# A new written order for the recurrence of a gated linear-attention and mixture-of-experts kernel, with ten more fill products

## Chip, cores, metric

One core of one Trainium2 chip. The metric is device microseconds (us) of one execution; lower is better. The engines are TensorE (PE; its weight loads are PEld), VectorE (DVE), ScalarE (ACT), GpSimd (POOL) and SyncE (SP), which here only issues DMAs.

## What is computed

```python
f = sigmoid(f_logit)                      # (B, H, S, D) = (4, 8, 768, 48), float32
for t in range(S):                        # one 48x48 state per batch and head
    state = f[t][:, None] * state + outer(k[t], v[t])
    y[t]  = q[t] @ state
x = y as (B*S, H*D) = (3072, 384)
e = argmax(x @ w_gate)                    # 8 experts, w1: 384x1024, w2: 1024x384
out = softmax(x @ w_gate)[e] * (relu(x @ w1[e]) @ w2[e])
```

## The kernel before, in words

**Units.** The recurrence is done in chunks of 128 tokens. Twelve units (0 to 11) hold one chunk of two batches each; even units and odd units follow each other in time through a state. Each unit has 8 segments of 128 partitions x 128 tokens: half `a` is segments 0 to 3, `b` is 4 to 7, and `c` to `f` are quarters (c, d make a; e, f make b). For a unit, ACT computes `exp` and `ln` of the logits (L684, L693), DVE a running sum (`sum`, L700), ACT two exponentials of it (`r`, L715/L717; `dec`, L730). The keys are multiplied by `r` (on POOL as `kr`, on DVE as `krv`, both L721), the queries by `dec` on DVE (`q`, L743). PE turns the keys (`kp`, L650 into tile tr), makes scores (`sc`, L647 into s), DVE masks them (`mx`, L775), PE multiplies them into the values (`wi`, L647 into yt), adds the older state's share (`bef`) and makes the unit's own state (`dp`); ACT copies turned keys out of PSUM (`keep`, L786), and the outputs (`set`, L857); DVE and POOL update the state (`upd`, L846/L848; with p, L850).

**Routing.** PE turns the outputs back to token rows (`xp`, `lay` on ACT copies them, L942), makes logits (`lo`), DVE picks the expert (`lg`, `oh`, `place`, `rec`), PE counts (`cnt`), and POOL scatters 128 rows at a time to their expert's region in memory (`send`, L260). `soon`, `turn`, `wide` load, turn and multiply the first rows of experts 0 and 1 ahead of time. Behind the recurrence come two second products of those rows (L456), then the experts, one after another, with weights loaded two ahead.

**What sets the order.** Nothing is scheduled by a planner at run time: `FIRST_STEPS` (L552) is a text of steps that the loop at L1106 carries out one by one, and every engine gets its instructions in the order of that text and runs them in that order. A step that waits holds up all that stands behind it on its engine. Loads (`lf`, `lk`, `lq`, `lv` of a unit; `lw`, `lww` first and second weights of an expert; `consts0` the 32 KB mask, `consts1` the other constants) are issued by SP in the text's order, each behind the last ACT step that stands before it in the text (`paced`, L657). `fill16` is 16 products of a zero tile into a bank that is written anew later (`warm`, L950): they compute nothing. A product of 128x128 float32 shows as two PE records.

**Buffers that tie engines together.** Scores go to two PSUM banks in turn, `kp`, `dp`, `xp` and `cnt` to a ring of two (L629), so each waits until the reader of the one before last (ACT's `keep` or `lay`, DVE's `upd` or `lg`) is done. The buffer of `r` is single.

```python
def paced(load):
    if "act" in done:
        tc.add_manual_dep(load.ins, done["act"].name, SYNC, ...)
def warm(count):
    for _ in range(count):
        nc.tensor.matmul(yt[0][:, 0], lhsT=pad[:, 0:C], rhs=pad[:, 0:C], start=True, stop=True)
for what, u, part in re.findall(r"([a-z]+)(\d+)([a-fp]?)", FIRST_STEPS):
    DO[what](int(u), part)
```

Of the kernel before, what the change touches and what calls it, by code (L numbers as in the profile page):

```python
# [170 lines left out]
def kernel(  # L171
# [366 lines left out]
    def load_pads(e):  # L538
# [11 lines left out]
        tc.add_to_no_dep_group("xs", ins)  # L550

    FIRST_STEPS = """  # L552
        lf0d lf1a lf0f lf0c lf0e lk0a exp0d ln0d lf1b lq0a lk0b sum0d exp1a ln1a exp0c exp0f
        exp0e consts0 lq0b lf2 ln0c sum0c ln0f sum0f sum1a ln0e sum0e lq1 exp1b lf3 r0c fill16
        r0f fill8 dec0f krv0c kp0c ln1b r0d sum1b dec0c lv0 r0e krv0d dec0e lk1 q0f krv0e dec1a
        q0c lv1 exp2 krv0f kp0d q0e dec0d q0d ln2 keep0a r1a sel0 lf4 r1b kp0e q1a kp0f keep0b
        lk2 sc0c sc0d sc0e last0 sc0f lk3 dec1b exp3 ln3 dp0 lq2 sum2 dec2 mx0a mx0b wi0a set0a
        lf5 kr1a kp1a upd0 last1 gate0 q1b consts1 sum3 kr1b kp1b r2 keep1a keep1b exp4 kr2b
        sc1a sc1b wi0b set0b lv2 lv3 ln4 kr2a dp1 mx1a wi1a set1a last2 line0 xp0b mx1b wi1b lq3
        upd1 lay0b q2 upd1p line1 line2 line3 line4 kp2b dec3 last3 lf6 sum4 set1b kp2a keep2a  # L560
        keep2b lq4 sc2a mx2a sc2b r3 xp0a xp1a lo1 wi2a mx2b krv3 lg1 lay0a lk4 wi2b q3 upd0p
        dp2 exp5 bef2 ln5 sum5 lq5 lay1a dec4 sc3a upd2 q4 mx3a kp3b lf7 exp6 line5 kp3a lk5
        sc3b set2a keep3b last4 r4 keep3a mx3b dp3 upd3 upd2p lv4 xp1b lv5 dec5 wi3a lk6 q5
        set2b wi3b ln6 kr4a kp4a lay1b kr4b r5 keep4a kr5a kp4b sc4a lf8 sum6 sc4b exp7 keep4b
        mx4a xp2b mx4b bef3 lk7 ln7 sum7 sc5a lq6 last5 lq7 lay2b kr5b sc5b r6 kr6b dp4 set3a
        kr6a lf9 set3b lv6 xp3a upd4 exp8 lo3 kp5b mx5a pads0 lg3 wi4a wi4b dec6 q6 last6 upd4p
        lay3a keep5b oh3 dec7 q7 lf10 r7 kr7b kp5a xp3b lay3b bef4 keep5a sc6a lk8 cnt3 ex3
        set4b mx5b place3 kr7a lq8 upd3p mx6a rec3 lv7 last7 ln8 xp2a set4a sc6b lay2a dp5 exp9
        upd5 send0 wi5a kp6a kp6b wi5b bef5 lk9 lq9 ln9 sum8 keep6b keep6a dp6 sum9 dec8 send0
        last8 lf11 sc7a upd6 set5a kp7b set5b mx6b r8 kp7a wi6a keep7b upd5p q8 keep7a lw0 wi6b  # L570
        upd6p send0 kr8b exp10 xp4a send0 xp5a ln10 mx7a lay4a lo5 lg5 dec9 sc7b oh5 lay5a bef6
        set6a xp4b lay4b xp5b kr8a mx7b wi7a q9 lay5b set6b lv8 r9 exp11 cnt5 place5 send0 lv9
        ex5 dp7 upd7 wi7b ln11 kr9a upd7p sc8a kp8b keep8b mx8a send0 kp8a lk10 bef7 sc8b sc9a
        lq11 set7a rec5 send0 xp6b keep8a line6 line7 dp8 lay6b sum10 kr9b wi8a mx8b send0 upd8
        set7b lk11 lq10 xp6a lay6a kp9a wi8b keep9a r10 mx9a xp7a sum11 lv10 kp9b send0 keep9b
        lo7 bef8 sc9b dec11 upd8p lg7 lay7a send0 oh7 lww0 lv11 mx9b kr10a dp9 send0 set8b kr10b
        xp7b set8a wi9a upd9 wi9b send0 dec10 soon0 lay7b q10 cnt7 line8 line9 ex7 xp8a lay8a
        bef9 set9a sc10a lw1 set9b sc10b place7 r11 q11 xp8b mx10a kr11b xp9a lo9 lay8b rec7
        send0 kr11a xp9b mx10b lg9 lay9b wi10a send0 wi10b bef10 set10a oh9 sc11a lay9a sc11b
        set10b cnt9 send0 mx11a mx11b xp10a lo10 turn0 last9 upd9p line10 send0 wi11a lg10  # L580
        place9 oh10 lay10a wi11b bef11 set11a ex9 rec9 xp10b lay10b send0 wide0 cnt10 send0
        set11b ex10 rec10 place10 xp11a lww1 line11 lo11 send0 xp11b lay11a lay11b turn1 lg11
        oh11 send0 ex11 rec11 wide1 send0 cnt11 last10 last11 place11 send0 wide2 send0 wide3
        send0
    """

    with ExitStack() as st:
# [1222 lines left out]
```

## Time and profile before

| | |
|---|---|
| runs | 359.98, 360.91, 361.52 us (median 360.91) |
| profiled execution | 362.03 us, of which the span of the trace is 360.3 us |
| recurrence and routing | to about 126 us of the span; then the experts |
| mean granted TensorE clock | 0.987 |

Times in the rows below are us from the start of the span. A timeline row gives start, duration, engine, line, operation, tiles written<-read, shape and count (x), and in brackets the idle time of the engine before it with what ended it.

### The profile page before, as it was taken

How to read it: one execution, taken by the hardware profiler on the slowest of the kernel's cores; microseconds unless marked ns; L12 is line 12 of the kernel's file. 1: busy time of each engine (PE TensorE's matmuls, PEld its weight loads, DVE VectorE, ACT ScalarE, POOL GpSimd, SP SyncE). 2: the span in 40 equal slices, each digit the busy share in tenths (PEclk: the TensorE clock that was granted, in tenths of full speed). 3: DMA queues.
4: the chain of work that ended last, by engine and by line, in shares of the span. 5: the costliest groups of instructions: out<-in, count | busy, mean ns of one | idle time of the engine just before them, and what ended most of it. 6: DMA issues, size and time to landing. Idle time of an engine off the chain costs nothing.

```text
span 360.3 us, 10263 instructions
## 1 busy us (share of the span) xinstructions
PE 344.2 (96%) x3962; PEld 295.4 (82%) x3962; DVE 275.7 (77%) x487; ACT 172.9 (48%) x372; POOL 247.5 (69%) x273
## 2 busy tenths in 40 slices
PE   8699998999999999999999999999999999999993
PEld 8488887888889868999997797896996896599682
DVE  5899989888984847489677858868978967977840
ACT  6999897876623211551443254155245234335310
POOL 6064785785875689699997499399485989935122
PEclk9799999999999999999999999999999999999998
DMA  6999879788948944999982899799179999980241
GB/s 196 359 324 351 291 256 358 262 295 315 323 130 279 366 116 116 311 291 371 391 300 64 268 387 338 216 365 376 36 183 384 226 349 389 372 305 17 70 153 47
DMA packets 57352, 94.97 MB, mean 264 GB/s; under 512 B 21016, under 2 KB 41307, under 8 KB 56272
## 3 DMA queue, kind: packets, MB, share of 16 engines
q1 hardware_dynamic: 54128, 84.60, 70.9%
q0 software_dynamic: 3168, 9.64, 7.0%
q8 instruction: 33, 0.54, 0.6%
q14 instruction: 23, 0.19, 0.2%
HBM read 79.22 MB, written 15.21 MB: 262 GB/s over the span
## 4 chain that ended last, share of the span: by engine, by line
PE 74%; DMA 8%; POOL 7%; issue 3%; ACT 3%; DVE 1%; SPq 1%; another core or an unknown queue 1%; POOLq 0%; ACTq 0%
PE hps L1404 15%; PE yps L1462 14%; PE yt L647 9%; PE tr L650 6%; PE yps L1279 6%; PE s L647 5%; DMA w2t<-in_moe_w_dram 4%; PE tr L647 4%; PE hps L436 3%; POOL was L1307 3%; PE hps L1256 2%; PE hps L1462 2%; DMA w1t<-in_moe_w_dram 2%; POOL w1t L1307 2%; POOL wsum L1298 2%
## 5 line engine op out<-in xcount | busy, mean ns | idle before, releaser
L260 POOL DMA_INDIRECT out_dram<-ysb,dst x26 | 28.5, 1096 | 48.2 <-DVE ysb L1480 22.5
L1422 ACT ACTIVATE hT<-hT 128x352 f32<-128x352 f32 (+1 forms) x48 | 23.9, 506 | 38.3 <-DVE hT L1392 38.1
L260 POOL DMA_INDIRECT xs<-xr,posi x24 | 27.4, 1140 | 19.0 <-issue 6.0
L1462 PE MATMUL yps<-w2t,hT 128*128 128x192 f32 x224 | 39.1, 328 | 0.0
L1462 PEld LDWEIGHTS yps<-w2t,hT 128*128 128x128 f32 x224 | 36.6, 190 | 3.0 <-issue 2.5
L1404 PE MATMUL hps<-xbs,w1t 128*128 128x176 f32 (+2 forms) x216 | 35.7, 309 | 0.3 <-POOL w1t L1307 0.3
L1307 POOL TENSOR_TENSOR was<-w1t 128x256 f32<-128x256 f32 x35 | 29.6, 863 | 7.4 <-DMA w1t<-in_moe_w_dram 3.8
L721 POOL TENSOR_TENSOR k<-k,r 128x512 f32<-128x512 f32 x20 | 28.3, 1424 | 8.6 <-ACT r L717 5.3
L1392 DVE TENSOR_TENSOR hT<-hps,hT 128x352 f32<-128x352 f32 (+1 forms) x42 | 22.2, 529 | 15.5 <-PE hps L1404 9.9
L1404 PEld LDWEIGHTS hps<-xbs,w1t 128*128 128x128 f32 x216 | 32.5, 190 | 0.6 <-issue 0.5
L1415 ACT COPY hT<-hps 128x352 f32<-128x352 f32 (+1 forms) x54 | 24.8, 459 | 16.7 <-PE hps L1404 4.7
L775 DVE COPY_PREDICATED at<-mpack,s 128x1024 f32<-128x1024 uint8 x24 | 31.1, 1316 | 1.6 <-PE s L647 1.5
L700 DVE TENSOR_TENSOR_SCAN sum<-g,cap 128x1032 f32<-128x1032 f32 (+2 forms) x16 | 27.7, 1754 | 3.9 <-ACT g L693 3.9
L1279 PE MATMUL yps<-qw,hqT 128*32 128x192 f32 (+1 forms) x192 | 27.5, 381 | 0.4 <-issue 0.2
L1307 POOL TENSOR_TENSOR w1t<-w1t 128x256 f32<-128x256 f32 x28 | 25.9, 925 | 0.6
L647 PE MATMUL yt<-at,v 128*48 128x128 f32 x384 | 24.3, 275 | 0.1
L647 PE MATMUL s<-q,k 64*64 64x128 f32 (+1 forms) x768 | 23.0, 261 | 0.9 <-issue 0.8
L647 PEld LDWEIGHTS s<-q,k 64*64 64x64 f32 x768 | 20.7, 141 | 3.0 <-issue 2.5
L1404 PE MATMUL hps<-xbs,was 128*128 128x176 f32 (+2 forms) x120 | 21.5, 310 | 0.5 <-ACT hold L1415 0.5
L647 PEld LDWEIGHTS yt<-at,v 128*48 128x48 f32 x384 | 20.2, 123 | 2.1 <-issue 1.2
L1279 PE MATMUL yps<-w2t,hT 128*32 128x384 f32 x192 | 21.4, 487 | 0.0
L1476 ACT ACTIVATE held<-yps,tg 128x192 f32<-128x192 f32 x24 | 10.1, 420 | 21.7 <-PE yps L1462 21.7
(187 smaller groups left out, 857.5 us busy)
## 6 DMA issues: line engine op xcount, KB each, us to landing
w1t<-in_moe_w_dram SPq DMA_DIRECT2D x8, 1536.0 KB
w2t<-in_moe_w_dram SPq DMA_DIRECT2D x8, 1536.0 KB
qw<-in_moe_w_dram SPq DMA_DIRECT2D x16, 768.0 KB
qw<-in_moe_w_dram SPq DMA_DIRECT2D x8, 1536.0 KB
q<-in_qu_dram SPq DMA_DIRECT2D x11, 512.0 KB
k<-in_ku_dram SPq DMA_DIRECT2D x11, 512.0 KB
f<-in_fu_dram SPq DMA_DIRECT2D x10, 512.0 KB
xs<-pad SPq DMA_DIRECT2D x8, 600.0 KB
```

What stands on the lines that cost most here:

```text
L260: ins = nc.gpsimd.indirect_dma_start(out=dst, out_offset=bass.IndirectOffsetOnAxis(ap=idx, axis=0), in_=src, in_offset=None, bounds_check= ...
L647: done["pe"] = nc.tensor.matmul(*a, **k).ins
L700: nc.vector.tensor_tensor_scan(x["sum"][:, part].rearrange("p s c -> p (s c)"), x["g"][:, part].rearrange("p s c -> p (s c)"), cap[:, part ...
L721: ins = on.tensor_tensor(k, k, units[u]["r"][:, part], op=OP.mult).ins
L775: nc.vector.copy_predicated(all_of(x["at"][:, a]), causal, all_of(x["ps", a]))
L1279: nc.tensor.matmul(yp[r], lhsT=h[:, f, at : at + T], rhs=w[:, f, cols], start=f == order[0], stop=f == order[-1], skip_group_check=True,)
L1307: on.tensor_tensor(to, first[1], second[1], op=op)
L1392: nc.vector.tensor_tensor(place(to), one, place(other), op=op)
L1404: nc.tensor.matmul(banks[n][:, g], lhsT=lhs[:, C * g : C * g + C], rhs=rhs, start=op == "new" and g == 0, stop=True, skip_group_check=True,)
L1415: nc.scalar.copy(place(more[0]), banks[n])
L1422: nc.scalar.activation(place(n), place(n), AF.Relu, scale=scale)
L1462: nc.tensor.matmul(to, lhsT=h[:, f], rhs=w[:, f], start=start and f == 0, stop=f == HB - 1, skip_group_check=True,)
```

## The change

Only the text `FIRST_STEPS` changes. All steps are the same and on the same engines, but in another order on every queue; `fill8` becomes `fill14`, and two steps `fill2` are new, so 34 products of zeros instead of 24. What stands first on each engine, before and after:

```
PE before   fill16 fill8 kp0c kp0d kp0e kp0f sc0c sc0d sc0e sc0f dp0 wi0a kp1a kp1b sc1a sc1b wi0b dp1 wi1a xp0b wi1b
PE after    fill16 fill14 kp0c fill2 sc0c fill2 sc0d kp0e kp0d kp0f sc0e sc0f dp0 kp1a wi0a kp1b wi0b sc1a sc1b xp0a dp1 wi1a
ACT before  exp0d ln0d exp1a ln1a exp0c exp0f exp0e ln0c ln0f ln0e exp1b r0c r0f dec0f ln1b r0d dec0c r0e dec0e dec1a exp2
            dec0d ln2 keep0a r1a r1b keep0b dec1b exp3
ACT after   exp0d ln0d exp0c exp0f exp0e ln0f ln0e ln0c exp1a exp1b ln1a r0d r0c ln1b r0e dec0d dec0c dec0f dec0e r0f exp2
            ln2 r1a dec1b keep0b keep0a dec1a r1b exp3
DVE before  sum0d sum0c sum0f sum1a sum0e krv0c sum1b krv0d q0f krv0e q0c krv0f q0e q0d q1a sum2 mx0a mx0b upd0 q1b sum3
DVE after   sum0d sum0f sum0c sum0e sum1a krv0c krv0d krv0e q0c q0e q0f q0d sum1b krv0f sum2 mx0a mx0b upd0 q1b q1a sum3
SP before   lf0d lf1a lf0f lf0c lf0e lk0a lf1b lq0a lk0b consts0 lq0b lf2 lq1 lf3 lv0 lk1 lv1 lf4
SP after    lf0d lf0c lf0f lf0e lf1a lf1b lk0a lq0a lk0b lq0b lf2 lk1 lf3 lv0 consts0 lv1 lq1 consts1 lk2 lf4
```

The diff, cut to its first lines, to the lines around unit 6's loads, and to its end:

```diff
     FIRST_STEPS = """
-        lf0d lf1a lf0f lf0c lf0e lk0a exp0d ln0d lf1b lq0a lk0b sum0d exp1a ln1a exp0c exp0f
-        exp0e consts0 lq0b lf2 ln0c sum0c ln0f sum0f sum1a ln0e sum0e lq1 exp1b lf3 r0c fill16
-        r0f fill8 dec0f krv0c kp0c ln1b r0d sum1b dec0c lv0 r0e krv0d dec0e lk1 q0f krv0e dec1a
...
-        sc3b set2a keep3b last4 r4 keep3a mx3b dp3 upd3 upd2p lv4 xp1b lv5 dec5 wi3a lk6 q5
-        set2b wi3b ln6 kr4a kp4a lay1b kr4b r5 keep4a kr5a kp4b sc4a lf8 sum6 sc4b exp7 keep4b
-        mx4a xp2b mx4b bef3 lk7 ln7 sum7 sc5a lq6 last5 lq7 lay2b kr5b sc5b r6 kr6b dp4 set3a
...
-        place9 oh10 lay10a wi11b bef11 set11a ex9 rec9 xp10b lay10b send0 wide0 cnt10 send0
-        set11b ex10 rec10 place10 xp11a lww1 line11 lo11 send0 xp11b lay11a lay11b turn1 lg11
-        oh11 send0 ex11 rec11 wide1 send0 cnt11 last10 last11 place11 send0 wide2 send0 wide3
-        send0
+        lf0d lf0c lf0f lf0e lf1a lf1b lk0a exp0d ln0d lq0a fill16 lk0b exp0c exp0f exp0e sum0d
+        ln0f sum0f ln0e lq0b ln0c sum0c exp1a lf2 lk1 exp1b ln1a lf3 lv0 r0d consts0 sum0e r0c
+        sum1a ln1b krv0c lv1 krv0d r0e fill14 krv0e dec0d lq1 dec0c sel0 dec0f consts1 dec0e q0c
+        q0e q0f q0d sum1b r0f krv0f exp2 kp0c fill2 ln2 sc0c fill2 sc0d sum2 mx0a last0 kp0e
+        kp0d r1a dec1b kp0f sc0e sc0f mx0b keep0b keep0a dp0 upd0 lk2 lf4 dec1a r1b kr1a lq2
...
+        lv4 line3 wi2a lg1 r4 dp2 line4 upd2 upd1p sc3a mx3a lf7 sc3b ln5 mx3b lay1a exp6 sum5
+        ln6 sum6 lk5 xp0b lay0b kp3a keep3a lf8 bef2 set2a kr4a sc4a kp3b lv5 keep3b set2b dec5
+        last4 kr4b kp4b sc4b r5 kr5a lk6 q5 dp3 kr5b wi3a upd3 mx4a exp7 wi3b keep4b lf9 ln7
+        upd3p lq6 last5 bef3 set3a lq7 mx4b kp4a keep4a set3b sum7 xp2a r6 sc5a kr6a sc5b xp3a
+        lo3 line5 mx5a lg3 lay2a upd2p dec6 lk7 lv6 xp2b wi4a lay2b oh3 wi4b lay3a exp8 ln8 ex3
+        q6 last6 dp4 upd4 mx5b bef4 set4a pads0 kp5b keep5b lf10 xp3b wi5a lq8 sum8 lay3b cnt3
...
+        oh10 cnt10 send0 xp11a ex10 rec10 place10 last10 last11 lww1 line11 set11b lo11 xp11b
+        lay11a lay11b turn1 send0 lg11 oh11 send0 ex11 rec11 wide1 send0 cnt11 place11 send0
+        wide2 send0 wide3
     """
```

Later on ACT, after the change, these runs stand ahead of copies: `exp6 ln6 lay0b keep3a`, `exp8 ln8 ex3 set4a`, `ln9 ex5 exp10 set6a`, `exp11 ln11 lay6a lay7a`. Expert 1's first weights (`lw1`) and expert 0's second (`lww0`) change places around the early row loads (`soon0`): lw1 now ahead of them, lww0 behind. Behind `place11`, two sends stand instead of three.

## Rows read from the trace of the kernel before

**Rows 1.** The page: TensorE's busy time over the span (us, share, instructions), then its granted clock in 40 slices of 9 us, in tenths.
```profile
PE 344.2 (96%) x3962; PEld 295.4 (82%) x3962; DVE 275.7 (77%) x487; ACT 172.9 (48%) x372; POOL 247.5 (69%) x273
PEclk9799999999999999999999999999999999999998
```

**Rows 2.** Windows of 10 us, all engines. Columns: the stretch, its length, busy us (and instructions) of PE, PEld, DVE, ACT, POOL, granted clock, DMA share, GB/s.
```profile
0.00:10.00 10.00, 7.74 (x48) 7.58 (x48) 5.73 (x13) 6.55 (x20) 5.96 (x21) 1.00 0.71 210
10.00:20.00 10.00, 7.40 (x108) 5.78 (x110) 9.03 (x14) 9.97 (x26) 2.10 (x4) 0.66 0.93 350
20.00:30.00 10.00, 10.00 (x236) 8.75 (x236) 10.00 (x10) 9.88 (x18) 5.32 (x5) 1.00 0.99 329
30.00:40.00 10.00, 9.01 (x224) 7.98 (x216) 9.96 (x10) 8.54 (x15) 5.77 (x9) 1.00 0.96 338
40.00:50.00 10.00, 9.84 (x273) 8.91 (x272) 9.91 (x7) 9.31 (x17) 6.97 (x6) 1.00 0.75 255
80.00:90.00 10.00, 10.00 (x237) 8.64 (x236) 8.53 (x8) 6.25 (x11) 5.79 (x7) 1.00 0.86 306
```

**Rows 3.** Windows of 1 us, the same columns.
```profile
4.00:5.00 1.00, 1.00 (x7) 1.00 (x6) 0.69 (x1) 0.97 (x4) 1.00 (x1) 1.00 0.88 270
8.00:9.00 1.00, 1.00 (x11) 1.00 (x10) 1.00 (x2) 0.00 (x0) 0.00 (x0) 1.00 1.03 341
11.00:12.00 1.00, 0.11 (x2) 0.00 (x0) 0.60 (x1) 1.00 (x5) 0.00 (x0) 1.00 0.94 379
13.00:14.00 1.00, 0.99 (x4) 0.58 (x4) 1.00 (x4) 1.00 (x2) 0.00 (x0) 0.50 1.05 404
```

**Rows 4.** Timeline of PE, 0 to 60 us: the fills (L953), the first turnings (tr<-fpack,k), scores (s), state (tr<-v,kn), then turnings and scores of the second unit.
```profile
1.56 7.74 PE L953 MATMUL yt<-pad 128*128 128x128 f32 x48 [1.56 <-POOL wg L591]
10.70 0.41 PE L650 MATMUL tr<-fpack,k 128*128 128x128 f32 x2 [1.41 <-issue]
13.01 2.03 PE L650 MATMUL tr<-fpack,k 128*128 128x128 f32 x6 [1.90 <-DVE k L721]
14.97 3.69 PE L647 MATMUL s<-q,k 64*64 64x128 f32 x64
18.59 1.40 PE L647 MATMUL tr<-v,kn 128*48 128x48 f32 x32
20.80 1.09 PE L650 MATMUL tr<-fpack,k 128*128 128x128 f32 x8
21.82 1.57 PE L647 MATMUL s<-q,k 64*64 64x128 f32 x64
```

**Rows 5.** Timeline of DVE, 0 to 30 us: running sums (L700), keys (L721), queries (L743), first masks (L775).
```profile
7.07 2.99 DVE L700 TENSOR_TENSOR_SCAN sum<-g,cap 128x258 f32<-128x258 f32 x4 [2.09 <-ACT g L693]
10.18 0.42 DVE L721 TENSOR_TENSOR k<-k,r 128x256 f32<-128x256 f32 x1
11.40 1.23 DVE L700 TENSOR_TENSOR_SCAN sum<-g,cap 128x516 f32<-128x516 f32 x1 [0.80 <-ACT g L693]
12.55 0.40 DVE L721 TENSOR_TENSOR k<-k,r 128x256 f32<-128x256 f32 x1
12.87 0.42 DVE L743 TENSOR_TENSOR q<-q,g 128x256 f32<-128x256 f32 x1
15.63 2.30 DVE L700 TENSOR_TENSOR_SCAN sum<-g,cap 128x1032 f32<-128x1032 f32 x1
17.85 2.50 DVE L775 COPY_PREDICATED at<-mpack,s 128x1024 f32<-128x1024 uint8 x2
```

**Rows 6.** Timeline of ACT, 0 to 30 us: the first exp of unit 1 (the half a), exp of a quarter, three ln of quarters, the exp that waits, the first of the four instructions of r0c and r0f, the dec behind them, the first keep, the exp of a whole unit.
```profile
4.16 0.62 ACT L684 ACTIVATE g<-f 128x512 f32<-128x512 f32 x1
5.43 0.40 ACT L684 ACTIVATE g<-f 128x256 f32<-128x256 f32 x1
6.63 1.01 ACT L693 ACTIVATE g<-g 128x256 f32<-128x256 f32 x3
9.02 0.63 ACT L684 ACTIVATE g<-f 128x512 f32<-128x512 f32 x1 [1.38 <-DMA f<-in_fu_dram]
9.65 0.29 ACT L715 ACTIVATE r<-sum 128x128 f32<-128x128 f32 x1
10.45 0.40 ACT L730 ACTIVATE g<-sum 128x256 f32<-128x256 f32 x1
15.50 0.56 ACT L786 COPY kn<-tr 128x512 f32<-128x512 f32 x1
18.21 1.04 ACT L684 ACTIVATE g<-f 128x1024 f32<-128x1024 f32 x1
```

**Rows 7.** Timeline of DVE, 48 to 64 us: the queries of unit 6.
```profile
53.42 1.23 DVE L743 TENSOR_TENSOR q<-q,g 128x1024 f32<-128x1024 f32 x1 [1.14 <-DMA q<-in_qu_dram]
```

**Rows 8.** Timeline of PE, 0 to 128 us: the two longest waits between 50 and 100 us.
```profile
56.71 0.32 PE L647 MATMUL yt<-q,state 48*48 48x128 f32 x3 [0.46 <-issue]
62.29 1.03 PE L650 MATMUL tr<-fpack,k 128*128 128x128 f32 x8 [0.81 <-ACT g L693]
```

**Rows 9.** Timeline of POOL, 100 to 150 us: the last scatter.
```profile
123.16 1.40 POOL L260 DMA_INDIRECT xs<-xr,posi  x1 [0.30 <-issue]
```

**Rows 10.** Timeline of DVE, 100 to 150 us: expert 0's later rows are turned.
```profile
133.00 1.24 DVE L418 STREAM_TRANSPOSE xT<-xrow 128x768 f32<-128x768 f32 x1
```

**Rows 11.** Timeline of PE, 58 to 200 us: the product that reads them.
```profile
136.31 10.52 PE L436 MATMUL hps<-xT,w1t 128*128 128x256 f32 x48
```

More of the change, by code (lines that the diff above doesn't have):

```diff
@@ L552 @@
     FIRST_STEPS = """
-        lf0d lf1a lf0f lf0c lf0e lk0a exp0d ln0d lf1b lq0a lk0b sum0d exp1a ln1a exp0c exp0f
-        exp0e consts0 lq0b lf2 ln0c sum0c ln0f sum0f sum1a ln0e sum0e lq1 exp1b lf3 r0c fill16
-        r0f fill8 dec0f krv0c kp0c ln1b r0d sum1b dec0c lv0 r0e krv0d dec0e lk1 q0f krv0e dec1a
-        q0c lv1 exp2 krv0f kp0d q0e dec0d q0d ln2 keep0a r1a sel0 lf4 r1b kp0e q1a kp0f keep0b
-        lk2 sc0c sc0d sc0e last0 sc0f lk3 dec1b exp3 ln3 dp0 lq2 sum2 dec2 mx0a mx0b wi0a set0a
@@ L558 @@
[L558 to L562, printed above, removed]
-        sc3b set2a keep3b last4 r4 keep3a mx3b dp3 upd3 upd2p lv4 xp1b lv5 dec5 wi3a lk6 q5
@@ L564 @@
-        set2b wi3b ln6 kr4a kp4a lay1b kr4b r5 keep4a kr5a kp4b sc4a lf8 sum6 sc4b exp7 keep4b
-        mx4a xp2b mx4b bef3 lk7 ln7 sum7 sc5a lq6 last5 lq7 lay2b kr5b sc5b r6 kr6b dp4 set3a
[L566 to L580, printed above, removed]
-        place9 oh10 lay10a wi11b bef11 set11a ex9 rec9 xp10b lay10b send0 wide0 cnt10 send0
@@ new lines @@
+        kp0d r1a dec1b kp0f sc0e sc0f mx0b keep0b keep0a dp0 upd0 lk2 lf4 dec1a r1b kr1a lq2
+        kp1a wi0a exp3 ln3 dec2 kr1b lv2 kp1b gate0 set0a r2 last1 q1b q1a lk3 wi0b keep1a sc1a
+        sc1b line0 keep1b sum3 set0b mx1a lq3 xp0a lf5 exp4 lay0a dp1 ln4 wi1a set1a mx1b lq4
+        kr2b upd1 kr2a last2 kp2a dec3 last3 q2 wi1b kp2b lk4 keep2b sum4 lf6 upd0p keep2a set1b
+        r3 sc2a mx2a sc2b mx2b xp1b dec4 krv3 lq5 line1 line2 xp1a lo1 q3 lay1b q4 exp5 wi2b lv3
+        lv4 line3 wi2a lg1 r4 dp2 line4 upd2 upd1p sc3a mx3a lf7 sc3b ln5 mx3b lay1a exp6 sum5
@@ new lines @@
+        ln6 sum6 lk5 xp0b lay0b kp3a keep3a lf8 bef2 set2a kr4a sc4a kp3b lv5 keep3b set2b dec5
[3 more added lines that the diff above has]
+        q6 last6 dp4 upd4 mx5b bef4 set4a pads0 kp5b keep5b lf10 xp3b wi5a lq8 sum8 lay3b cnt3
+        place3 kr6b r7 set4b rec3 kp5a sc6a lk8 keep5a mx6a sc6b mx6b dec7 q7 kr7b send0 xp4a
@@ new lines @@
+        kp6b lay4a kr7a last7 lw0 wi5b send0 dp5 exp9 keep6b upd4p r8 kr8a kr8b bef5 set5a set5b
+        kp6a dec8 sc7a send0 upd5 lv7 sc7b mx7a xp5a lo5 lg5 keep6a oh5 lk9 xp5b wi6a lay5a
+        lay5b lq9 ln9 wi6b last8 ex5 cnt5 xp4b q8 send0 exp10 bef6 set6a place5 lv8 dp6 set6b
+        lay4b sum9 upd6 wi7a r9 send0 sc8a upd6p kp7a lf11 kp7b lk10 dec9 mx7b sc8b upd5p kr9b
+        wi7b line6 line7 rec5 q9 keep7b keep7a dp7 send0 kp8b bef7 ln10 lv9 upd7 lq11 keep8b
+        set7b kp8a set7a mx8a keep8a exp11 mx8b kr9a xp6a lq10 send0 sum10 ln11 lay6a sc9a xp7a
@@ new lines @@
+        lo7 lg7 sum11 send0 lv10 lay7a wi8a wi8b sc9b send0 r10 kr10b lk11 bef8 dp8 mx9b set8a
+        xp6b lv11 mx9a send0 upd7p set8b lw1 wi9a upd8 xp8b send0 lay6b dec10 oh7 ex7 kr10a
+        send0 kp9b rec7 line8 lay8b keep9b q10 wi9b xp7b lay7b upd8p dec11 bef9 cnt7 soon0
+        place7 line9 kp9a keep9a sc10a sc10b xp8a q11 mx10b send0 set9a set9b r11 kr11b xp9a
+        send0 lay8a lo9 dp9 wi10b mx10a lg9 lay9a wi10a kr11a send0 upd9 oh9 ex9 bef10 rec9 xp9b
+        lay9b sc11a sc11b mx11a cnt9 mx11b send0 place9 turn0 set10a xp10a set10b last9 upd9p
@@ L585 @@
+        lo10 send0 wi11a lww0 wi11b bef11 set11a xp10b line10 lg10 lay10a lay10b send0 wide0
+        oh10 cnt10 send0 xp11a ex10 rec10 place10 last10 last11 lww1 line11 set11b lo11 xp11b
+        lay11a lay11b turn1 send0 lg11 oh11 send0 ex11 rec11 wide1 send0 cnt11 place11 send0
+        wide2 send0 wide3
     """
```

## The prediction

> **What bounds the kernel now.** I read the page first: TensorE is busy 96% of the span and its granted clock is full except in the slices from 9 to 18 us and the last [rows 1]. The 10-us windows show two regimes in the recurrence [rows 2]. From 10 to 50 us VectorE is busy 9.03 to 10.00 of every 10 us and the loads keep the DMA engines at shares of 0.75 to 0.99; TensorE is nearly full too, but in 10 to 20 us it has 7.40 at a mean clock of 0.66. By 80 us it has turned: TensorE 10.00, VectorE 8.53. So an early saving counts only as far as VectorE has it too, and a late wait of TensorE counts in full.
>
> The 1-us windows show the clock [rows 3]: in 11 to 12 us TensorE works 0.11 us, and in 13 to 14 us its clock stands at 0.50, the lower level of 1.2 GHz. The timeline tells why it idled and what it cost [rows 4]: the fills end at 9.30, two turnings run at 10.70, the other six wait 1.90 for a key product on VectorE. Then six turnings take 2.03 (eight take 1.09 at full clock) and 64 score records 3.69 (later 1.57): 2.03 x 8/6 - 1.09 = 1.6 and 2.1, so 3.7 us.
>
> The wait has a chain. The key product at 12.55 stands on VectorE behind sum1b, which starts at 11.40 after 0.80 of waiting for ln1b [rows 5]; ln1b stands on ACT behind exp1b, which waited 1.38 for the load lf1b until 9.02 [rows 6].
>
> **Part by part.**
>
> **Loads.** lf1b moves ahead of lk0a and no longer waits for ln0d. It must be in by 7.6 (next part) where it was in at 9.02. Unit 0's and unit 1's logits are 1.05 MB together; at the 270 GB/s of 4 to 5 us [rows 3] they take 3.9 us from the first packets at about 2 us, so it can be there by 6 to 7. Bounds: no wait, or the old 1.38. I take none. In exchange lq1 now goes behind k1, f3, v0, the mask (consts0) and v1. Ahead of the mask stand 4.06 MB (seven unit loads of 0.52, and 0.39 of v0, by their shapes); 210 GB/s in the first 10 us and 350 in the next [rows 2] move that by 15.6 us. consts1 and other loads that come earlier fill SP's pauses and cost nothing there; if the queue is full they push q1 back.
>
> **ACT.** From 4.16, where ln0d is through: three quarter exps of 0.40, three ln in 1.01, two half exps of 0.63 make 7.6; ln1a 0.6; r0d and r0c 0.40 each (two r between 9.65 and 10.45) make 9.0; ln1b 0.6, r0e 0.40, four decs of about 0.33 make 11.3; r0f, exp2 and ln2 (1.04 each) make 13.8 [rows 6]. exp2 has moved from 13.21 to 11.7 at no cost, since the queue in front of it lost its wait.
>
> **VectorE.** A quarter sum is 0.6 (2.99 for five quarters), a key or query product 0.32 from start to start (12.55 to 12.87) [rows 5]. sum1a starts behind ln1a at 8.2 and ends at 9.4; krv0c, d, e end at 10.4; q0c waits for dec0c (10.6), q0e for dec0e (11.3), and q0d ends at 12.3; sum1b 1.23 and krv0f make 13.8. So sum2 starts at 13.8 and not at 15.63, but q1a (some 0.6) now stands behind it: the net lead is **1.2 us**. The first mask comes at 16.1, near to the mask's own arrival of 15.6, so part of the lead is at risk. Bounds 0 and 1.8; I take **1.0**.
>
> **TensorE.** 20 more fills are 40 records. Twelve of them precede kp0c; at 11 records per us [rows 3] they last 1.1 and end at 10.4, inside the idle stretch from 9.30 to 10.70: free. If krv0c came at 9.8, they would delay it by 0.6, still ahead of q0c at 10.9. The two fill2 (four records, 0.4 each) lie in the waits for q0c and q0d; without that cover they cost 0.8. With fills, turnings and scores spread over 9 to 13 us instead of 0.4 us of work, I expect the clock to stay full. sc0e and sc0f then end 0.9 behind krv0f, at about 14.8, and not at 18.59: 3.8 earlier. That is not banked. dp0 needs keep0a, which ACT reaches behind r1a, dec1b and keep0b, at about 16.2 (it was at 15.50, [rows 6]), so dp0 starts 2.4 earlier; and the products with masked scores need VectorE, which is only 1.0 ahead.
>
> In 20 to 30 us TensorE's matmul row says 10.00 of 10, its weight loads 8.75, VectorE 10.00 [rows 2]. The Trainium skill (Perfetto Trace Analysis, Identifying the Most-Contended Engine) says that matmul occupancy is a poor measure of TensorE's headroom and weight-load occupancy a better one, while VectorE's occupancy can be taken as it is. By the matmul row 2.4 to 3.8 us would be banked; by that rule VectorE's 1.0.
>
> **From 20 to 62 us.** The order of masks, sums and queries on VectorE changes, their sum does not. q6 waited 1.14 for its load [rows 7]. In the new order lq6 has as many loads in front of it, but q6 stands behind lg3 and oh3 (some 1.9 us of small steps), which cover a load of the old lateness. TensorE's waits at 56.71 and 62.29 (0.46 and 0.81, [rows 8]) stand just behind. If they go, 1.3 us are won; if the new order makes as many others, none; bounds -1.3 and 2.4 (1.14 and 1.27). I take **1.0**: the VectorE that was late is then early.
>
> **After 62 us.** No wait of TensorE between there and 100 us is as long as those two, so there is little to win. lw1 and lww0 change places; each 1.57 MB takes 4.5 us at 350 GB/s and both have over 10 us of cover until the second products at 126 us; if that were gone it would cost up to those 4.5. The end of the recurrence must carry the lead on: the last scatter (123.16, [rows 9]) lets the rows of expert 0 come, turned from 133.00 to 134.24 [rows 10] and read at 136.31 [rows 11]. That is 2.1 us of cover, and one send fewer behind the last routing (1.3 us of POOL) adds to it. I take 0.
>
> **Sum:** 1.0 + 1.0 = 2.0 us. The profiled execution took 362.03, so 360.0; the median stands 1.12 under it, so **358.9**.
>
> **Rivals.**
> 1. **The lead is eaten by loads.** VectorE is ready for its mask and queries before they are there: the DMA share is already 0.93 to 0.99 in 10 to 40 us [rows 2], and what comes earlier makes something else later. For it: the mask's 15.6 against 16.1. Against: the 1.14 us at q6 was the only such VectorE wait there. Left are 0 to 0.7 us: 360.4. Chance 0.26.
> 2. **The clock falls all the same**, because TensorE waits for q0c and q0d between the fills, or it falls a little later while dp0 waits. Then the 3.7 us stay lost, dp0 comes at about 18, and only VectorE's queue is ahead: 360.9 less 0 to 0.6, so 360.6. Against: work is spread over the stretch that was idle. Chance 0.10.
> 3. **TensorE is the bound already at 20 us.** Then the 2.4 us of dp0 are banked, with 1.3 of waits and 1 of the tail: 360.9 - 4.7 = 356.2. For it: its row is full. Against: VectorE's is too. Chance 0.09.
> 4. **ACT holds TensorE up: slower.** The wait of 0.81 at 62.29 ended with an ln of ACT [rows 8], where a copy out of the turning banks stands behind an exp and ln pair (2 x 1.04, [rows 6]). The new order has four such runs ahead of copies that free a bank or feed a turning (units 6, 8, 9/10 and 11). Each costs nothing as long as TensorE has 2.1 us of other work in front of it, and from there 0.8 to 2.1 us. All four at 0.8 less the early 1.0 give 360.9 + 2.3 = 363.2. Against: the old order has such pairs as well, and one wait. Chance 0.13.
>
> **How the numbers follow.** The forecast has 0.42 (its own range 357.4 to 359.9, from the bounds of its two terms at half). A measurement can tell 0.5%, which is 1.8 us: below 359.1 is faster, above 362.7 slower. Forecast and rival 3 make faster 0.51; rivals 1 and 2 make same 0.36; rival 4 makes slower 0.13. The forecast lies only 0.2 us beyond the bound, so faster and same are near to each other. The range reaches to rival 3 and over most of what lies between no change and rival 4: 356.0 to 362.4.
>
> **What would show it.** Clock 1.00 in 13 to 19 us, sc0f through by 15 to 16 us, VectorE's sum2 at about 13.8 and its first mask by 16.5 show the start right. The lead must then be read at unit 6's first mask and at the last score. Wrong, if the clock still drops before 20 us, if VectorE waits for a DMA between 10 and 20 us, or if TensorE has more than 1.5 us of new waits on ACT after 50 us.

## The result and the profile after

The changed kernel takes **365.78 us** (median of 4 runs, 364.68 to 368.62) against 360.74 for the one before (359.98 to 361.52): ratio **1.0137**, 95% interval 1.0096 to 1.0177. The forecast was 358.9, with 362.4 as the upper end. The profiled execution took 365.26 us with a span of 363.5.

The page answers to [rows 1]: the dip of the clock between 9 and 18 us is gone, and a new one stands in the eighth slice, 64 to 73 us. TensorE is busy 1.5 us longer in a span that is 3.2 longer.

```profile
PE 345.7 (95%) x3982; PEld 296.3 (82%) x3982; DVE 274.4 (75%) x487; ACT 173.0 (48%) x372; POOL 248.5 (68%) x273
PEclk9999999899999999999999999999999999999999
```

The 10-us windows of after, with the columns of [rows 2]. Clock 1.00 in the second row, where it was 0.66; but VectorE did no more in it (8.98 after 9.03). And 60 to 70 us, where the forecast saw little to win or lose, has TensorE at 7.22 and VectorE at 4.46.

```profile
10.00:20.00 10.00, 7.92 (x136) 6.28 (x137) 8.98 (x13) 9.30 (x24) 4.23 (x3) 1.00 0.98 352
...
60.00:70.00 10.00, 7.22 (x200) 6.38 (x193) 4.46 (x7) 5.08 (x10) 4.70 (x6) 0.95 0.81 304
70.00:80.00 10.00, 9.77 (x181) 7.94 (x179) 7.33 (x17) 6.44 (x13) 6.05 (x7) 0.88 0.62 209
```

Before, the stretch from 60 to 70 us had 9.19 and 8.97:

```profile
60.00:70.00 10.00, 9.19 (x205) 8.06 (x200) 8.97 (x9) 7.82 (x13) 5.47 (x7) 1.00 0.75 247
```

Timeline of PE, after (start, duration; answers to [rows 4], then to nothing that was shown): the scores of unit 0 end at 16.35 and not at 18.66. The first product for the state (dp0) waits 1.30 for ACT and starts at 17.66, where 16.2 was forecast. At 68.23 the scores of unit 7 come 2.78 after the turnings before them, waiting for a key product of GpSimd (kr7a). At 87.85 scores wait 0.80 for another.

```profile
14.88 0.44 PE L650 MATMUL tr<-fpack,k 128*128 128x128 f32 x2 [0.21 <-DVE k L721]
15.25 1.10 PE L647 MATMUL s<-q,k 64*64 64x128 f32 x32
17.66 0.93 PE L647 MATMUL tr<-v,kn 128*48 128x48 f32 x32 [1.30 <-ACT kn L786]
...
64.80 0.66 PE L650 MATMUL tr<-fpack,k 128*128 128x128 f32 x4
68.23 2.51 PE L647 MATMUL s<-q,k 64*64 64x128 f32 x64 [2.78 <-POOL k L721]
...
87.85 0.90 PE L647 MATMUL s<-q,k 64*64 64x128 f32 x32 [0.80 <-POOL k L721]
```

Timeline of DVE, after ([rows 5, 7]): sum2 starts at 15.54, forecast was 13.8, and waits 0.72 for ACT; the first mask is 0.08 earlier than before. The wait at q6 is gone. Unit 7's mask waits 5.35.

```profile
14.43 0.40 DVE L721 TENSOR_TENSOR k<-k,r 128x256 f32<-128x256 f32 x1
15.54 2.31 DVE L700 TENSOR_TENSOR_SCAN sum<-g,cap 128x1032 f32<-128x1032 f32 x1 [0.72 <-ACT g L693]
17.77 2.52 DVE L775 COPY_PREDICATED at<-mpack,s 128x1024 f32<-128x1024 uint8 x2
...
54.29 1.20 DVE L743 TENSOR_TENSOR q<-q,g 128x1024 f32<-128x1024 f32 x1
...
69.93 1.34 DVE L775 COPY_PREDICATED at<-mpack,s 128x1024 f32<-128x1024 uint8 x1 [5.35 <-PE s L647]
```

Timeline of ACT, after ([rows 6]): two exps wait for loads of logits, the last quarter of unit 0 and unit 2.

```profile
6.11 0.42 ACT L684 ACTIVATE g<-f 128x256 f32<-128x256 f32 x1 [1.14 <-DMA f<-in_fu_dram]
...
13.27 1.06 ACT L684 ACTIVATE g<-f 128x1024 f32<-128x1024 f32 x1 [0.64 <-DMA f<-in_fu_dram]
```

Now GpSimd around 60 us, where the new order puts the first scatter of the routed rows ahead of kr7a. Before, it stood still for 3.95 us in front of that scatter, with kr7a already done:

```profile
57.33 2.53 POOL L721 TENSOR_TENSOR k<-k,r 128x512 f32<-128x512 f32 x2
59.82 0.83 POOL L850 TENSOR_TENSOR state<-state,kept 128x384 f32<-128x384 f32 x1
60.59 0.20 POOL L738 COPY kept<-g 128x8 f32<-128x8 f32 x1
64.73 1.95 POOL L260 DMA_INDIRECT xs<-xr,posi  x1 [3.95 <-issue]
```

After, it stands still for 5.06, and kr7a (66.91) is behind it. "issue" and TensorE's turning are what the profile found last; neither was the cause (below).

```profile
59.23 1.41 POOL L721 TENSOR_TENSOR k<-k,r 128x512 f32<-128x512 f32 x1 [2.29 <-ACT r L717]
65.70 1.18 POOL L260 DMA_INDIRECT xs<-xr,posi  x1 [5.06 <-PE tr L650]
66.91 1.26 POOL L721 TENSOR_TENSOR k<-k,r 128x512 f32<-128x512 f32 x1
```

What it cost, in 1-us windows (columns as in [rows 3]): TensorE idles from 65.5 to 68.2, and soon after it starts again it works some 3.4 us at the lower level of its clock, 1.2 GHz.

```profile
66.00:67.00 1.00, 0.00 (x0) 0.00 (x0) 0.00 (x0) 0.00 (x0) 0.96 (x2) 1.00 1.01 430
...
68.00:69.00 1.00, 0.77 (x36) 0.77 (x39) 0.00 (x0) 0.79 (x2) 0.83 (x3) 0.96 0.62 251
69.00:70.00 1.00, 1.00 (x31) 0.87 (x26) 0.07 (x1) 1.00 (x3) 0.97 (x2) 0.50 0.18 60
70.00:71.00 1.00, 1.00 (x19) 0.88 (x17) 1.00 (x1) 1.00 (x2) 1.00 (x2) 0.50 0.52 200
71.00:72.00 1.00, 1.00 (x12) 0.65 (x14) 0.27 (x1) 0.76 (x2) 1.00 (x2) 0.50 0.06 13
72.00:73.00 1.00, 1.00 (x32) 0.78 (x24) 0.00 (x0) 0.00 (x0) 0.83 (x2) 0.83 0.56 135
```

So 2.78 of waiting, and 0.04 + 3 x 0.50 + 0.17 = 1.7 of clock (68 to 73 us): 4.5 in this execution. The wait of 0.80 at 87.85 is not part of that: it is there without the standstill too (experiments 2 and 3). The median rose by 5.0, the span of the two profiled executions by 3.2. The last scatter came at 127.08 (123.16, [rows 9]), the rows of expert 0 were turned at 137.10 ([rows 10]) and read at 140.45 ([rows 11]): 2.1 us of cover as before, so all stands some 4 us later in a row.

```profile
140.45 10.52 PE L436 MATMUL hps<-xT,w1t 128*128 128x256 f32 x48
```

### The profile page after: what moved, and what is told of

It is laid out like the page before. It is cut to its first block, busy times and chain, and to the rows that moved or that the text cites. A ratio compares the mean times of both kernels' runs of the same rounds, so it can differ in the third digit from the quotient of the medians.

```text
span 363.5 us, 10302 instructions
## 1 busy us (share of the span) xinstructions
PE 345.7 (95%) x3982; PEld 296.3 (82%) x3982; DVE 274.4 (75%) x487; ACT 173.0 (48%) x372; POOL 248.5 (68%) x273
## 4 chain that ended last, share of the span: by engine, by line
PE 79%; issue 5%; DVE 4%; DMA 4%; POOL 3%; ACT 3%; POOLq 1%; SPq 0%; DVEq 0%; ACTq 0%
PE hps L1404 22%; PE yps L1462 17%; PE yps L1279 7%; PE yt L647 6%; PE tr L650 3%; PE hps L1256 3%; PE s L436 3%; PE s L647 3%; PE yps L456 3%; PE hps L1462 3%; PE hps L436 3%; DMA q<-in_qu_dram 2%; PE tr L647 2%; DVE sum L700 2%; PE yt L456 1%
## 5 line engine op out<-in xcount | busy, mean ns | idle before, releaser
L721 POOL TENSOR_TENSOR k<-k,r 128x512 f32<-128x512 f32 x20 | 28.6, 1438 | 16.7 <-ACT r L717 13.4
L260 POOL DMA_INDIRECT xs<-xr,posi x24 | 25.3, 1054 | 19.2 <-PE tr L650 6.6
L775 DVE COPY_PREDICATED at<-mpack,s 128x1024 f32<-128x1024 uint8 x24 | 30.4, 1312 | 7.0 <-PE s L647 6.9
L1307 POOL TENSOR_TENSOR was<-w1t 128x256 f32<-128x256 f32 x35 | 28.5, 829 | 8.3 <-DMA xs<-xr,posi 4.2
L700 DVE TENSOR_TENSOR_SCAN sum<-g,cap 128x1032 f32<-128x1032 f32 (+2 forms) x16 | 28.1, 1772 | 4.2 <-ACT g L693 4.2
L647 PE MATMUL s<-q,k 64*64 64x128 f32 (+1 forms) x768 | 21.8, 256 | 3.8 <-POOL k L721 3.6
L647 PEld LDWEIGHTS s<-q,k 64*64 64x64 f32 x768 | 18.9, 137 | 6.9 <-POOL k L721 4.4
```

Source lines behind the costliest of these rows:

```text
L260: ins = nc.gpsimd.indirect_dma_start(out=dst, out_offset=bass.IndirectOffsetOnAxis(ap=idx, axis=0), in_=src, in_offset=None, bounds_check= ...
L647: done["pe"] = nc.tensor.matmul(*a, **k).ins
L700: nc.vector.tensor_tensor_scan(x["sum"][:, part].rearrange("p s c -> p (s c)"), x["g"][:, part].rearrange("p s c -> p (s c)"), cap[:, part ...
L721: ins = on.tensor_tensor(k, k, units[u]["r"][:, part], op=OP.mult).ins
L775: nc.vector.copy_predicated(all_of(x["at"][:, a]), causal, all_of(x["ps", a]))
L1307: on.tensor_tensor(to, first[1], second[1], op=op)
```

## The experiments

Each ratio is to the kernel before, run side by side on the same chip. The first four ran on one chip, where before takes 360.4 us; 5 to 8, 9 to 12, 13, and 14 and 15 ran on four others, where it takes 357.6 to 358.1. Between these groups ratios are compared, not times. Added lines move the line numbers by one or two.

**Theories.** A: the first scatter of an execution costs GpSimd 4 to 5 us, wherever it stands. B: it waited for TensorE. C: no single step is at fault, the order is worse as a whole. D, added later: GpSimd's instruction stream runs dry at a place that is counted in instructions.

**1. The first send behind kr7a**, the rest as after.

```
- ... r7 ... kr7b send0 xp4a kp6b lay4a kr7a last7 lw0 ...
+ ... r7 ... kr7b xp4a kp6b lay4a kr7a last7 send0 lw0 ...
```

> The changed kernel, but the first scatter stands behind kr7a and last7 on GpSimd instead of ahead of kr7a. Theory A (the first scatter of an execution holds GpSimd for 4 to 5 us before it starts, whatever it waits for: 3.95 us of idle time before it in the kernel before, 5.06 in the changed one): kr7a starts at about 61 us and not at 66.9, sc7a's wait of 2.78 us goes, the 4 to 5 us of idle time stay in front of the scatter at its new place, and the time falls by 4 to 5 us to about 361. Theory B (the scatter waited for TensorE's turning kp6a, which ended at 65.45): the time falls likewise, but the idle time in front of the first scatter falls below 1.5 us, since at its new place its own PE step is kp6b. Rival C (the loss comes from the order as a whole, loads and masks): the time stays within 1 us of 365.8.

Measured: 362.74, ratio 1.0056 (1.0025 to 1.0088). The standstill is there, but kr7a is now ahead of it, and TensorE's wait of 2.78 is gone:

```profile
58.92 2.55 POOL L721 TENSOR_TENSOR k<-k,r 128x512 f32<-128x512 f32 x2 [2.89 <-ACT r L717]
61.41 0.20 POOL L738 COPY kept<-g 128x8 f32<-128x8 f32 x1
65.56 1.18 POOL L260 DMA_INDIRECT xs<-xr,posi  x1 [3.95 <-PE tr L650]
```

One step moved in GpSimd's queue gives back 0.8% (2.9 us), less than the 4 to 5 us that A and B expected. C falls as the main cause. B asked for less than 1.5 us of standing still here, and 3.95 remain: B falls.

**2 and 3. An early scatter of nothing** (all its indices out of bounds) at about 7 us, where GpSimd is idle: in after, and in before.

```
+ nowhere = cpool.tile([128, 1], I32, name="nowhere")
+ nc.gpsimd.memset(nowhere, FAR)
+ "first": lambda u, p: scatter(xs, nowhere, pad, ROWS - 1, "xs"),
- ... sel0 ...
+ ... sel0 first0 ...
```

> The changed kernel with one more scatter, whose 128 indices all lie out of bounds so that it writes nothing, on GpSimd behind sel0, where GpSimd is idle from 6 to 12 us. Theory A: that scatter takes the 4 to 5 us of first-time cost where GpSimd has nothing to do; the first real scatter then starts within 1 us of its data, kr7a starts at about 62 us, sc7a waits under 0.3 us, and the time is 360 to 361. Theory B: the real scatter still waits until about 65.5 us, sc7a still waits 2 to 3 us, and the time stays at 365 to 366.

> The kernel before with the same extra scatter of nothing behind sel0. Theory A: the 3.95 us of idle time in front of its first real scatter (64.73 us) fall under 1 us, that scatter starts at about 61 us; as nothing urgent stood behind it, the time stays within 1 us of 360.7. Theory B: the idle time stays at about 4 us. Either way no slower than 361.8.

Measured: after with it 360.5, ratio 1.0007 (0.9984 to 1.0031); before with it 359.69, ratio **0.9962** (0.9934 to 0.9989), faster than both kernels. Both lost the standstill in front of the first routed scatter. In after with the early scatter:

```profile
7.16 1.37 POOL L262 DMA_INDIRECT xs<-pad,nowhere  x1 [0.18 <-issue]
...
58.37 1.34 POOL L723 TENSOR_TENSOR k<-k,r 128x512 f32<-128x512 f32 x1 [2.19 <-ACT r L719]
60.56 1.04 POOL L262 DMA_INDIRECT xs<-xr,posi  x1 [0.84 <-PE s L649]
```

In before with it, where the scatter itself now takes 2.98 and not 1.95, so that part of the standstill may still be in it:

```profile
61.47 2.98 POOL L262 DMA_INDIRECT xs<-xr,posi  x1 [0.54 <-issue]
```

A looked right, but the early scatter itself waited only 0.18: if it had cost 4 to 5 us, they were hidden behind GpSimd's memsets of the first 6 us, or it never cost them.

One wait of TensorE on GpSimd is left in after with the early scatter, 0.80 at 82.56. There kr9a stands behind a scatter in GpSimd's queue:

```profile
82.56 0.90 PE L649 MATMUL s<-q,k 64*64 64x128 f32 x32 [0.80 <-POOL k L723]
```

All twelve traces of the new order have this wait (0.67 to 0.81), with and without the standstill; none of the five of the old order has it.

**4. Before, with kr7a behind the first send.**

```
- ... place3 kr7a lq8 upd3p ... send0 ...
+ ... place3 lq8 upd3p ... send0 kr7a ...
```

> The kernel before with the single step kr7a moved behind the first scatter on GpSimd (it stood ahead of it). Theory A: kr7a starts behind the scatter at about 66.7 us instead of 58.6 and ends at 68; kp7a and sc7a, which came at 67.5 and 66.1, wait about 2 us, and the time rises by 2 to 4 us to 363 to 365: most of the measured loss from this one position. Rival C: the time stays within 1 us of 360.7.

Measured: 361.22, ratio 1.0029 (0.9999 to 1.0058). That is 0.85 us above before in the same runs: within C's 1 us, and not A's 2 to 4. TensorE waits 1.42 for kr7a. The standstill had changed shape with kr7a no longer ahead of it: 1.92 in front of the scatter, and the scatter (2.77) and kr7a (2.24) long themselves.

```profile
61.41 2.77 POOL L260 DMA_INDIRECT xs<-xr,posi  x1 [1.92 <-issue]
64.21 2.24 POOL L721 TENSOR_TENSOR k<-k,r 128x512 f32<-128x512 f32 x1
```

So the loss from this one position alone is small here, and a standstill that changes with what stands ahead of it speaks against A; that led to D.

**5. Twelve small memsets and no scatter** at 7 us, in after.

```
+ "small": lambda u, p: [nc.gpsimd.memset(idle, 0.0) for i in range(u)],
- ... sel0 ...
+ ... sel0 small12 ...
```

> After, with twelve memsets of one column on GpSimd behind sel0 (at about 7 us, where it is idle) and no early scatter. Two theories of the 4 to 5 us in which GpSimd stands still in front of the first routed scatter. A: the first scatter of an execution costs it that, whatever else GpSimd did. D: it is GpSimd's instruction stream that runs dry there; an 8 KB packet of the queue of instructions starts 1.8 to 2.2 us before each stall ends (62.61 and 64.49 before, 63.31 and 65.53 after), and an extra scatter only moved the place at which it runs dry. A: the stall stays, 5 us in front of the first scatter, and the time is that of after, 365.8 (+-1). D: twelve more instructions move the place too; no idle stretch over 2 us in front of the first scatter, or one at another instruction, and the time falls toward 360.5 to 362.

Measured: 357.87, ratio 1.0021 (0.9982 to 1.0060), where after had 1.0137. The first scatter comes after 0.64 of idle time:

```profile
57.79 1.82 POOL L722 TENSOR_TENSOR k<-k,r 128x512 f32<-128x512 f32 x1 [1.72 <-ACT r L718]
60.25 1.18 POOL L261 DMA_INDIRECT xs<-xr,posi  x1 [0.64 <-PE tr L651]
```

**6. The scatter of nothing at 27 us** instead, behind kr2a and TensorE's scores (the step first0 behind kr2a).

> After, with the scatter of nothing not at 7 us but behind kr2a (it ends at 26.7 us), waiting for TensorE's latest scores so that GpSimd comes to it with nothing else running long. A: 3 to 5 us of standing still show there, between kr2a and last2 at 28.7, and none in front of the first routed scatter at 60 us; the time 360.5 to 363, by what unit 1's update loses. D: nothing shows at 27 us, the scatter itself is 1 to 1.4 us; at 60 us the stall may be there or not, by where the stream runs dry.

Measured: 358.66, ratio 1.0021 (0.9980 to 1.0061). The scatter started after 1.40 of idle time and took 1.97, where the later one of run 2 took 1.04: at most 1.40 + 0.93 = 2.3 us, where A asked for 3 to 5. The standstill at 60 us is gone here too, with the stream longer by the scatter's own instructions.

```profile
27.61 1.97 POOL L262 DMA_INDIRECT xs<-pad,nowhere  x1 [1.40 <-PE yt L649]
```

**7 and 8. The fills alone**: after with the early scatter and the old fills (fill16, fill8); before with the early scatter and more fills (fill14 for fill8, and a fill8 behind kp0c).

> The after kernel with the early scatter of nothing (so without the stall), and the fills of before: fill16 and fill8, no fill2. Against the same kernel with the new fills (360.5, ratio 1.0007 in its own runs). If the fills' full clock between 10 and 20 us is worth what TensorE saves there (2.4 to 3.8 us), this is 362.5 to 364. If VectorE is the bound up to 50 us, as I had it, the fills are worth 0 to 1: 360 to 361.5, with the clock at half in 12 to 19 us and VectorE's sum2 and first mask where they were.

> The before kernel with the early scatter of nothing (359.69, ratio 0.9962 in its own runs), and more fills in the old order: fill14 for fill8, and a fill8 behind kp0c, in the 1.4 and 1.9 us in which TensorE waits there. The clock part of the change alone. Banked: the clock stays full to 20 us, sc0f ends 2 to 3.7 us earlier, and 356 to 358 comes out. VectorE the bound: the scores end earlier all the same, the first mask does not, 359 to 360.

Measured: 358.36, ratio 1.0018 (0.9983 to 1.0052), against 1.0007 for the same kernel with the new fills (run 2); and 359.05, ratio 1.0019 (0.9979 to 1.0060), against 0.9962 without the added fills (run 3); runs 2 and 3 were on another chip. So the clock was moved as meant (0.66 in 10 to 20 us in the one, 1.00 in the other), and neither shows a gain from the fills; one of the 2.4 to 3.8 us that TensorE saves (0.7 to 1.1%) would have shown, and a smaller one lies within the intervals. In the second, scores end at 16.4 where they ended at 18.7, and then TensorE waits 0.80 for VectorE's masks.

```profile
14.15 2.28 PE L649 MATMUL s<-q,k 64*64 64x128 f32 x64
...
18.92 1.08 PE L649 MATMUL yt<-at,v 128*48 128x128 f32 x16 [0.80 <-DVE at L777]
```

**9 to 12. A dose, and two controls.** After unchanged, on another chip; four memsets (small4); the twelve memsets behind kr7a, and so behind the first scatter; the twelve at 7 us in before.

> The after kernel itself, unchanged, beside the three below, because the twelve small memsets were timed on a chip on which before took 357.7 and not 360.4. The stall should be there: 4 to 5 us of standing still in front of the first scatter, TensorE's wait of 2 to 3 us behind it, and a ratio of 1.010 to 1.018. Without the stall here, the memsets have shown nothing.

> After, with four small memsets on GpSimd behind sel0 instead of twelve. D (the instruction stream runs dry at a place that is counted in instructions): four records more move the place in front of kr7b, where GpSimd waits for ACT anyway, as the early scatter did with its four or five records; no 4 us in front of the first scatter, ratio near 1.001. A (the first scatter's own cost): the stall as in after, ratio 1.010 to 1.018.

> After, with the twelve small memsets behind kr7a, so behind the first scatter in GpSimd's queue. D: nothing in front of the first scatter has moved in the stream, so the stall of 4 to 5 us stays and the ratio is 1.010 to 1.020. If memsets as such (their use of GpSimd, or chance from one build to the next) had taken it away, it goes here too.

> Before, with the twelve small memsets behind sel0. D: its 3.95 us in front of the first scatter go too, and what they cost it: 0.994 to 0.999, as the early scatter gave (0.9962). A: 3.95 us stay, 0.999 to 1.002.

| kernel | idle before the first routed scatter, us | ratio (95%) |
|---|---|---|
| after unchanged | 6.13 | 1.0099 (1.0058 to 1.0141) |
| after, 4 memsets ahead | 3.00 | 1.0032 (0.9996 to 1.0067) |
| after, 12 ahead (5.) | 0.64 | 1.0021 (0.9982 to 1.0060) |
| after, 12 behind | 5.25 | 1.0201 (1.0137 to 1.0265) |
| before, 12 ahead | 0.67 (3.95 without) | 0.9974 (0.9943 to 1.0005) |

The first scatter of these, in this order (the third stands above):

```profile
66.00 1.18 POOL L260 DMA_INDIRECT xs<-xr,posi  x1 [6.13 <-issue]
```

```profile
62.74 1.30 POOL L261 DMA_INDIRECT xs<-xr,posi  x1 [3.00 <-PE tr L648]
```

```profile
64.36 1.18 POOL L261 DMA_INDIRECT xs<-xr,posi  x1 [5.25 <-issue]
```

```profile
60.96 2.99 POOL L261 DMA_INDIRECT xs<-xr,posi  x1 [0.67 <-issue]
```

A falls: instructions that have nothing to do with a scatter take the standstill away, and only if they are ahead of it. Four of them halve it, where I had expected none to be left. So the standstill depends on what stands ahead in GpSimd's stream, as D says, but a count of instructions alone does not fit. The first routed scatter is GpSimd's 70th record in after; the early scatter put three records ahead of it and left 0.84, four memsets left 3.00. Whether a scatter stands for more instructions than the trace records, no run shows.

Two things in the table stay open. With the twelve behind, the kernel is slower than after unchanged on the same chip (1.0201 against 1.0099); why was not tested. And in before with twelve ahead the scatter itself takes 2.99, as in run 3, and the interval reaches 1.0005.

That it is the fetch of instructions is not shown. The DMA view speaks for it; its row is queue, kind, packets, MB, share. In after, one packet of the instruction queue starts between 60.5 and 65.5 us (at 63.31; GpSimd goes on at 65.53):

```profile
q14 instruction: 1, 0.01, 1.2%
```

With twelve memsets ahead, that queue has no packet between 55 and 66 us, and two between 50 and 55 (the first of them is there in after too, at 55.00):

```profile
q14 instruction: 2, 0.02, 0.8%
```

That this packet is GpSimd's is inferred from its moving 10 to 11 us earlier when GpSimd alone got twelve more instructions (in after from 63.31 to 53.56, in before from 62.61 to 51.22). In runs 2 and 3, with the early scatter, the packet came at 60.8 and 59.2 and nothing stood still for 2 us in front of the scatter, so its time alone does not tell where GpSimd stops.

**13 to 15. Unit 2's logits earlier**, since in after, without the standstill too, sum2 waits for ln2 and exp2 for f2. All with the twelve memsets ahead: lf2 behind lq0a; lf2 behind exp0e; and none of it.

> After with the twelve small memsets ahead of the first scatter (so without the stall), and unit 2's logits f2 loaded 0.52 MB earlier: behind q0a and so ahead of k0b and q0b. In the run with the memsets alone (ratio 1.0021) ACT's exp2 waits 1.24 for f2 until 12.90 and VectorE's sum2 1.31 for ln2 until 15.17, so the lead that I forecast at sum2 went there. Theory L (f2's arrival took it): exp2 starts by 11.7 to 12.0, sum2 by 13.9 to 14.3, the first mask by 16.1 to 16.5 (it was 17.39), the lead of about 1 us is carried to 50 us, and the ratio falls by 0.002 to 0.003 to about 0.999. Theory W (the loads are the bound whatever their order): k0b or q0b, then k1 or q1 become late by the 1.5 us, the first mask comes at 17.0 or later or the lead is gone at unit 1, and the ratio stays at 1.001 to 1.004.

> After with the twelve small memsets ahead of the first scatter, and f2's load moved up to just behind exp0e, the last reader of unit 0's logits in the same buffer: ahead of q0b, and issued at about 6 us where it was issued at 6.93 (8.18 in the first profile of after). In the run that put it behind q0a the load overwrote those logits, so exp0c to exp0e waited 7.1 us for it and took unit 2's; this one is the order that was meant. Theory L (f2's arrival took the lead): exp2 1.0 to 1.5 earlier (11.4 to 12.0), sum2 at 13.9 to 14.3 and the first mask at 16.1 to 16.6, against 12.90, 15.17 and 17.39; carried on, the time falls by 0.7 to 1.2 us under the control of this job. Theory W (the loads are the bound in any order): q0b, k1 or q1 become late by as much, the lead is gone by unit 1's first mask (24.13), and the time is within 0.5 us of the control.

> The control beside it: after with the twelve small memsets and nothing else, as timed before (ratio 1.0021). Ratio 1.000 to 1.004; no standstill over 1 us in front of the first scatter; sum2 at 15.2 to 15.6 behind a wait for f2, by either theory.

Measured: 364.27, ratio 1.0148 (1.0108 to 1.0187); 358.76, ratio 1.0037 (1.0009 to 1.0065); control 359.23, ratio 1.0035 (1.0009 to 1.0060). The first of them says nothing on L or W: f2 lands in the buffer of unit 0's logits while three quarters of these are unread, so those quarters are computed from unit 2's, the kernel computes something else, and ACT stands still for 7.11 us. In the second, exp2 no longer waits for a load, but it starts at 12.91 all the same, and sum2 at 15.17, where the control has 14.84 (the exp2 of the second, then of the control):

```profile
12.91 1.04 ACT L685 ACTIVATE g<-f 128x1024 f32<-128x1024 f32 x1
```

```profile
12.57 1.06 ACT L685 ACTIVATE g<-f 128x1024 f32<-128x1024 f32 x1 [0.97 <-DMA f<-in_fu_dram]
```

The times are within 0.5 us of each other, as W had it, but neither L nor W is shown. In the second the exp of unit 0's last quarter waited 0.98 for its own load, which is issued ahead of f2, and made all behind it on ACT late; the control had no such wait. One trace of each cannot tell this from the move of f2. The lead of 0.8 us that the control has over before at its first mask (17.07 against 17.85) is gone by unit 1's (24.04 against 23.73).

## Why the prediction was wrong

**The step that failed** is the one after 62 us, "there is little to win", taken as 0. It asked which waits of TensorE the new order could take away, and not what the moved sends put in front of its key products. The diff moves the first send ahead of kr7a on GpSimd's queue, and the trace of before had the row: 3.95 us of standing still ahead of that scatter, nearly harmless because kr7a was done (0.26 to 0.38% in runs 12 and 3). The price was there to read; the forecast priced sends for the last routing only. Measured: 1.30% between after and after with the early scatter (4.7 us), 0.64 to 0.78% between after (run 9) and after with twelve memsets (runs 15 and 5) on the other chips (2.3 to 2.8 us). None of the signs that the prediction named would have pointed to GpSimd.

**VectorE's lead, forecast 1.0, did not last.** The step "exp2 has moved from 13.21 to 11.7 at no cost" counted ACT's queue and not the load behind it. In the ten traces of the new order with f2's load in its place, exp2 starts between 12.57 and 13.29, and in nine of them it waits 0.31 to 1.24 for f2. This is rival 1's mechanism, at f2 instead of the mask that it named. sum2 starts between 14.84 and 15.56 in these ten, against 15.35 to 16.14 in the five of the old order; 13.8 was never reached. At unit 1's first mask the two orders are level, 23.53 to 24.39 and 23.56 to 24.29. That an earlier f2 would have kept the lead is not shown (13 to 15).

**The clock and the fills** went as forecast in kind: 1.00 in 10 to 20 us (0.91 to 1.00 in the other traces of the new order with its fills), and the scores earlier, though by 2.3 us and not 3.8. That this banks nothing of its size also held (experiments 7 and 8); that VectorE is the bound there fits TensorE's wait of 0.80 for its masks in run 8. So rivals 2 and 3 fall.

**The waits at 53 to 62 us, forecast 1.0:** q6's went, but TensorE got one of 1.50 at 45 us, so at most part of it was won.

**Rival 4** named the wrong engine: after the change no wait of TensorE on ACT between 50 and 126 us is over 0.3 us. A slower outcome came, by a wait on GpSimd that no rival named.

**Without the standstill** on either side, the new order is still no faster: 1.0007 against 0.9962, and 1.0021 to 1.0035 against 0.9974, so 1.6 to 2.2 us by the ratios (0.8 by the medians of the first pair), with intervals that overlap or nearly do. TensorE's wait of 0.67 to 0.81 for kr9a, which only the new order has, can be part of that; it was not tested alone, and the rest stays open.

**Two slips in the numbers** changed nothing: the change adds ten products of zeros, 20 records (3982 against 3962), where the prediction has 20 and 40; and halfway from its two terms to their bounds gives 357.8 to 360.6, not 357.4 to 359.9.

## What to carry to other kernels

Before a step is moved ahead of another on an engine's queue, read how long that engine stands still in front of it in the trace of before: a long idle row with "issue" or an unlikely releaser is a price that lies hidden until something urgent is queued behind it. A lead that is worked out from one engine's queue must be checked against the arrival of every load that this queue reads. Some cheap instructions ahead of such a standstill are worth a trial: here twelve memsets took it away in both orders, though in before the gain (0.26%) is within the noise.

## What the runs showed of the hardware

GpSimd stood still for 3.95 to 6.13 us in front of the first routed scatter, in both orders, and what stood ahead of it in its stream decided how long: 0.64 to 0.67 us with twelve memsets ahead, 3.00 with four, 5.25 with the twelve behind. The cause of the standstill stays open. The Trainium skill (Runtime: NRT & Kernel Launch, Instruction fetch mechanics) says that an engine's sequencer fetches the next page over a DMA queue of its own, and that crossing a boundary is mostly hidden; if the packets that start at 62.61 and 63.31 are that fetch, it was not hidden here. The same skill (GPSIMD Engine Reference, Instruction dispatch) has about 6 us for the first call to freshly loaded code, with no visible instruction; its size fits, but memsets alone removed the standstill, and a first scatter at 27 us cost 2.3 us at most. After 2.78 us without work and some 0.7 us of work at full clock, TensorE's granted clock was 0.50 from 69 to 72 us.
